# Attention's stores of x behind its loads, a new order within a batch, and ranks, lanes and scatter positions at other places

## The chip, the core and the metric

The kernel runs on one core of one Trainium2 chip. The metric is the device time of one execution in microseconds (us). Engines: TensorE (PE, its weight loads PEld), VectorE (DVE), ScalarE (ACT), GpSimd (POOL) and SyncE (SP, which here issues DMAs).

## What is computed

```python
# q, k, v: (8, 8, 576, 64); the attention has no softmax
kv = einsum('bhsd,bhse->bhde', k, v)
out = einsum('bhsd,bhde->bhse', q, kv)
x = out / sqrt(mean(out * out, -1) + 1e-6) * g_norm     # -> x: (4608, 512), one row per token
logits = x @ w_gate + modality_bias[modality_id]        # 8 experts
e_idx = argmax(logits, axis=1)
for e in range(8):                                      # F = 1024
    h = relu(x[e_idx == e] @ w1[e])
    y[e_idx == e] = gate_w[e_idx == e] * (h @ w2[e])
gate = 1 / (1 + exp(-(y @ w_gate2)))
result = (gate * (y @ w_val)) @ w_out                   # d_ff = 1536
```

## The kernel before, in words

There are three stages. Attention (lines 141 to 519) makes x, chooses each token's expert and numbers the tokens by expert. The expert stage (589 to 832) gathers the rows of x by that numbering, in 26 items of one or two tiles of 128 tokens, and multiplies them with w1 and w2. The last stage (836 to 953) is the gated pair of products. All matrix products but the routing's counts are in full precision, made of split high and low parts.

The order is written out by hand: each engine executes its instructions in the order of the code, and waits at an instruction whose data or buffer is not there. SP's queue issues nearly all loads and stores, in the order of the code too.

Attention works batch by batch (line 376). For batch b, `emit_kv` (234) makes the product of k and v on PE ("kv", 72 products) and VectorE copies it into a block R. `emit_RT` (247) transposes R on PE into PSUM (rtp), VectorE copies that to SBUF (rt), and `emit_M` (254) multiplies rt with the router's weights (mp) and copies the result into the last 16 columns of R. `emit_qT` (261) transposes a quarter of q (qc, a copy of q in another layout; in odd batches a fifth piece qr with the rest of two batches), and ScalarE copies it to one of five qT buffers. `emit_out` (269) multiplies qT with R: x not yet normed and the router's raw logits at once; ScalarE copies it to o and squares it (sq), VectorE sums the squares (ssq). The outputs of batch b are made while batch b+1 is under way, piece r by piece r. One pass of the loop before:

- kv of batch b at the start, then for each r: out(b-1, r), the transposition of R (r = 0), qT(b, r), M (r = 2);
- loads of batch b+2 at r = 1, `norm` (286) of batch b-2 and the store of x of batch b-4 (`store_x`, 368);
- in odd passes `choose` (309: expert of each token as a one-hot, oh), in the even pass after the next odd one `rank` (323: the place of each token within its expert, by matmuls of oh with a triangle and with ones), `lanes` (350: a one-hot of the place within 128, lo) and `numbers` (357: lo times the token's number, two rows of lid per tile).

The loads' buffers are double: k and v of batch b+2 can be loaded when kv(b) has read them. The x buffers o are three for even and two for odd batches. A DMA on SP's or ScalarE's queue has one of eight semaphores in turn, and waits until the DMA eight places before it has landed.

Behind the loop come the last norm, choose and rank, then (439 to 503) a chain of small instructions on VectorE that turns the experts' counts into a code for each of 44 slots (sc); its comparison with each token's code (soh) and 72 products with lid (ph) give the token that stands in each place of a slot. From that come gidx (492), the rows that the gathers read, and est (503), the experts of the items. Lines 508 to 519 make sidx, the rows that the scatters of y write; the first scatter comes when the first item is done. `split_w` and line 438 split weights into high part (ScalarE, w1h) and low part (VectorE, w1l, 486).

Of the kernel before, what the change touches and what calls it, by code (L numbers as in the profile page):

```python
# [23 lines left out]
E = 8  # L24
# [10 lines left out]
C_U, C_IOTA, C_TOK, C_DESC, C_POS, C_REST, C_ITEM, C_CODE, C_ID, C_W = 0, 128, 256, 328, 336, 380, 381, 407, 432, 560  # L35
# [11 lines left out]
def shape_constants():  # L47
# [12 lines left out]
    c[:, C_TOK:C_TOK + NTILE] = (tok + 1) // 128  # L60
# [4 lines left out]
    e = 160 - NTILE * (E - np.arange(E))  # L65
    c[:, C_CODE:C_CODE + 18] = [*e, 200, *e, 200]
# [5 lines left out]
def attention_moe_glu_kernel(  # L72
# [68 lines left out]
    with ExitStack() as st:  # L141
# [29 lines left out]
        code = big.tile([128, NTILE], BF16, name="code")  # L171
# [21 lines left out]

        load_kv(0)
# [5 lines left out]
        load_q(0)  # L200
        load_kv(1)
        load_q(1)
# [13 lines left out]
        nc.vector.memset(onesb, 1.0)  # L216
        nc.vector.memset(tot[:, 0, :], 0.0)
# [14 lines left out]
        qT, o_t, me_t = {}, {}, {}  # L232
# [76 lines left out]
        def choose(bp):  # L309
# [4 lines left out]
            me = me_t[bp] = sm.tile([128, 9], F32, tag="me", name="me")  # L314
# [8 lines left out]
        def rank(bp):  # L323

            t0, n = 9 * bp, 9
            og = oh[:, t0:t0 + n, :]
            tr = sm.tile([128, 8], F32, tag="tr", name="tr")
            nc.vector.tensor_reduce(out=tr, in_=og.rearrange("p t e -> p e t"), op=ALU.add, axis=AX)
            nc.vector.tensor_tensor(out=tot[:, bp + 1, :], in0=tot[:, bp, :], in1=tr, op=ALU.add)
# [20 lines left out]
        def lanes(bp, lane):  # L350

            bc = [128, 9, 128]
            lo = wk.tile(bc, BF16, tag="lo", name="lo", bufs=1)
            nc.vector.tensor_tensor(out=lo, in0=iotab.unsqueeze(1).broadcast_to(bc), in1=lane.unsqueeze(2).broadcast_to(bc), op=ALU.is_equal)
            return lo

        def numbers(bp, lo, act):

            t0, n, bc = 9 * bp, 9, [128, 9, 128]
            for w in range(2):  # L360
                c = w * NTILE + t0
                if act:
                    for t in range(n):
                        nc.scalar.activation(out=lid[:, t0 + t, w, :], in_=lo[:, t, :], func=ACTF.Copy, scale=ct[:, C_TOK + c + t:C_TOK + c + t + 1])
                else:
                    nc.gpsimd.tensor_tensor(out=lid[:, t0:t0 + n, w, :], in0=lo, in1=tokb[:, c:c + n].unsqueeze(2).broadcast_to(bc), op=ALU.mult)
# [9 lines left out]
        for b in range(B + 1):  # L376
            if b < B:
                qc = wk.tile([128, 4, H, D], F32, tag="qc", name="qc", bufs=1)
                nc.scalar.activation(out=qc[:, 0], in_=q_t[b][:, :, 0, :], func=ACTF.Copy)
                emit_kv(b)  # L380
            if b == 0:
                make_bias()
            for r in range(5):
                if b == B and r == 0:
                    ld_scope.close()
                    mw = [mw_scope.enter_context(tc.tile_pool(name="m_wr0", bufs=1, side="right", reuse_waits="tile"))]
                    w1p = w1_scope.enter_context(tc.tile_pool(name="m_w1", bufs=3, side="right", reuse_waits="tile"))
                    w1r = [mw[0].tile([128, KC, F1], F32, tag="w1r0", name="w1r0")]
                    w2r = [mw[0].tile([128, F1 // 128, DM], F32, tag="w2r0", name="w2r0")]
                    nc.sync.dma_start(out=w1r[0], in_=w1[0].rearrange("(c p) f -> p c f", p=128))  # L390
                if b < B and r == 0:
                    nc.scalar.activation(out=qc[:, 1], in_=q_t[b][:, :, 1, :], func=ACTF.Copy)
                    for i in (2, 3):
                        nc.gpsimd.tensor_copy(out=qc[:, i], in_=q_t[b][:, :, i, :])
                if b:
                    emit_out(b - 1, r)
                if b < B:
                    if r == 0:
                        emit_RT(b)
                    if r < 4:  # L400
                        emit_qT((b, r), qc[:, r].rearrange("p h d -> p (h d)"))
                    elif b % 2:
                        emit_qT((b, 4), qr_t[b // 2].rearrange("p h d -> p (h d)"))
                    if r == 2:
                        emit_M(b)
                if r == 1:
                    load_kv(b + 2)
                    load_q(b + 2)
                    if b > 1:
                        norm(b - 2)  # L410
                    if b > 3:
                        store_x(b - 4)
                if b % 2 and b > 1:
                    if r == 3:
                        choose(b // 2 - 1)
                elif b > 2:
                    if r == 1:
                        lane = rank(b // 2 - 2)
                    elif r == 3:
                        lo = lanes(b // 2 - 2, lane)  # L420
                        if b < B:
                            numbers(b // 2 - 2, lo, False)
# [5 lines left out]
        numbers(2, lo, True)  # L428
# [5 lines left out]
        nc.tensor.matmul(out=tp, lhsT=onesb, rhs=tot[:, 4, :], start=True, stop=True)  # L434
        numbers(3, lanes(3, lane), True)
        w1s = {(0, 0): [w1p.tile([128, KC, 256], F32R, tag="w1" + z, name="w1" + z) for z in "hl"]}
        wq = w1r[0][:, :, 0:256]
        nc.scalar.activation(out=w1s[0, 0][0], in_=wq, func=ACTF.Copy)
        ti = big.tile([128, 8], I32, name="ti")
        tw = big.tile([128, 2, 8], I32, name="tw")  # L440
        seg = big.tile([128, 18], F32, name="seg")
        off = big.tile([128, 18], F32, name="off")
        dlt = big.tile([128, 17], F32, name="dlt")
        cnt = big.tile([128, 17], F32, name="cnt")
        pad = big.tile([128, 17], F32, name="pad")
        cmp, cm2 = (wk.tile([128, 512], F32, tag="rt", name=z)[:, 0:NITEM * 17].rearrange("p (t g) -> p t g", g=17) for z in ("cmp", "cm2"))
        itc, itp = (big.tile([128, NITEM], F32, name=z) for z in ("itc", "itp"))
        sc = big.tile([128, NSLOT], BF16, name="sc")
# [25 lines left out]
        for i in range(2):  # L474
            nc.vector.tensor_scalar(out=pairs[:, :, i], in0=itc[:, 0:NPAIR], scalar1=float(i), scalar2=None, op0=ALU.add)
        nc.vector.tensor_copy(out=sc[:, 2 * NPAIR:], in_=itc[:, NPAIR:])
        ph = [pq.tile([128, 512], F32, tag="q", name="php") for _ in range(2)]
        for t0 in range(0, NTILE, 9):
# [8 lines left out]
        vv = big.tile([128, NSLOT], F32, name="vv")  # L487
        v1 = big.tile([128, NSLOT], F32, name="v1")
        v2 = big.tile([128, NSLOT], F32, name="v2")
# [17 lines left out]

# [3 lines left out]
        nc.vector.tensor_tensor(out=pad, in0=seg[:, 1:18], in1=seg[:, 0:17], op=ALU.subtract)  # L511
        nc.vector.scalar_tensor_tensor(out=pad, in0=pad, scalar=128.0, in1=cnt, op0=ALU.mult, op1=ALU.subtract)
        nc.vector.tensor_tensor(out=cm2, in0=cmp, in1=pad.unsqueeze(1).broadcast_to([128, NITEM, 17]), op=ALU.mult)
        nc.vector.tensor_reduce(out=itp, in_=cm2, op=ALU.add, axis=AX)
        pos, v1p = (z[:, 0:2 * NPAIR].rearrange("p (t i) -> p t i", i=2) for z in (ct[:, C_POS:C_POS + NSLOT], v1))
# [464 lines left out]
```

## Time and profile before

| | us |
|---|---|
| median of 3 runs | 1585.08 (1582.66 to 1587.09) |
| the profiled execution | 1581.24, its span 1579.5 |
| kv of batch 0 starts on PE | 12.98 |
| first out of batch 7 on PE | 120.51 |
| last norm starts on VectorE | 132.62 |
| gidx is ready | 149.89 |
| first gathered tile is normed | 154.53 |
| PE busy over the span | 1509.2 (96%) |

The profile is of one execution; times inside it count from the start of its span. Busy time is that in which the engine executes; the granted clock (PEclk) is a mean over a stretch, 1.00 for 2.4 GHz throughout. A releaser is what the profile takes for the end of a wait; "issue" stands where it shows none. Durations on VectorE and ScalarE overlap a little with the next instruction's start.

### The profile page before, as it was taken

The page shows a single profiled execution, that of the slowest core. Times are in us where ns is not written, and L with a number is a line of the kernel's source. Part 1 is how long each engine was busy: PE and PEld are TensorE (multiplying, and loading weights), DVE is VectorE, ACT ScalarE, POOL GpSimd, SP SyncE. Part 2 cuts the span into 40 slices and gives each one's busy share as a digit, 9 for nine tenths or more (in the row PEclk, how much of TensorE's full clock was granted, in tenths as well). Part 3 has the DMA queues.
Part 4 walks back from the last instruction along what each step waited for, and adds up shares of the span by engine and source line. Part 5 has one row for each costly group of instructions (what it writes and reads, how often), then busy time and mean ns, then how long its engine had stood idle before and what let it go on. Part 6 is the DMA issues. An engine that isn't in the chain of part 4 may idle for free.

```text
span 1579.5 us, 22828 instructions
## 1 busy us (share of the span) xinstructions
PE 1509.2 (96%) x9089; PEld 1298.1 (82%) x9089; DVE 839.0 (53%) x1306; ACT 716.0 (45%) x1147; POOL 380.7 (24%) x418
## 2 busy tenths in 40 slices
PE   6993999999999999989999999999999999999997
PEld 6982899999999999767888888888888888888885
DVE  2558778878878878575333433333333333333322
ACT  3755555555555556533333433333333343333332
POOL 1031112222222213131311414114132141231211
PEclk9996999999999999999999999999999999999999
DMA  9976787757784778350000000000000000000000
GB/s 304 334 273 229 197 281 272 283 190 276 266 308 164 264 269 289 134 209 28 27 1 28 27 28 27 1 28 28 26 29 1 28 27 1 27 1 1 27 1 27
DMA packets 78877, 195.86 MB, mean 124 GB/s; under 512 B 13872, under 2 KB 22320, under 8 KB 75824
## 3 DMA queue, kind: packets, MB, share of 16 engines
q1 hardware_dynamic: 63984, 153.55, 28.5%
q0 software_dynamic: 12064, 40.46, 7.1%
q8 instruction: 74, 1.21, 0.3%
q10 hardware_dynamic: 2720, 0.35, 0.2%
q14 instruction: 35, 0.29, 0.1%
HBM read 177.08 MB, written 38.23 MB: 136 GB/s over the span
## 4 chain that ended last, share of the span: by engine, by line
PE 89%; DMA 4%; DVE 4%; issue 1%; ACT 1%; POOL 1%; POOLq 0%; SPq 0%; DVEq 0%; ACTq 0%
PE gv L576 12%; PE gv L578 12%; PE gv L577 12%; PE ac L895 6%; PE ac L897 6%; PE ac L896 6%; PE ph L672 5%; PE ph L671 5%; PE ph L670 5%; PE py L692 5%; PE py L693 5%; PE py L694 4%; PE kv L241 2%; PE ops L278 2%; DMA y_d<-y,sidx 2%; PE xtp L655 1%
## 5 line engine op out<-in xcount | busy, mean ns | idle before, releaser
L576 PE MATMUL gv<-yh,gvh 128*128 128x512 f32 x848 | 336.0, 396 | 0.0
L578 PE MATMUL gv<-yh,gvl 128*128 128x512 f32 x848 | 332.6, 392 | 2.0 <-DVE gvl L570 2.0
L577 PE MATMUL gv<-yl,gvh 128*128 128x512 f32 x848 | 331.2, 391 | 0.0
L580 DVE TENSOR_TENSOR gm<-sg,gv 128x512 f32<-128x512 f32 x107 | 73.5, 687 | 411.8 <-PE gv L578 410.1
L873 POOL TENSOR_TENSOR wol<-wlast,woh 128x512 fp32r<-128x512 f32 x72 | 100.0, 1389 | 475.0 <-ACT woh L872 475.0
L581 ACT ACTIVATE gh<-gm 128x512 fp32r<-128x512 f32 x107 | 67.6, 632 | 312.1 <-DVE gm L580 312.1
L670 PE MATMUL ph<-xh,w1h 128*128 128x256 f32 (+1 forms) x704 | 201.9, 287 | 0.8 <-ACT xh L659 0.8
L672 PE MATMUL ph<-xl,w1h 128*128 128x256 f32 (+1 forms) x704 | 199.5, 283 | 0.0
L671 PE MATMUL ph<-xh,w1l 128*128 128x256 f32 (+1 forms) x704 | 199.2, 283 | 0.0
L578 PEld LDWEIGHTS gv<-yh,gvl 128*128 128x128 f32 x848 | 159.5, 188 | 38.4 <-DVE gvl L570 2.9
L577 PEld LDWEIGHTS gv<-yl,gvh 128*128 128x128 f32 x848 | 159.7, 188 | 33.3
L576 PEld LDWEIGHTS gv<-yh,gvh 128*128 128x128 f32 x848 | 160.0, 189 | 32.1
L895 PE MATMUL ac<-woh,gh 128*128 128x512 f32 x428 | 168.2, 393 | 0.0
L897 PE MATMUL ac<-woh,gl 128*128 128x512 f32 x428 | 167.9, 392 | 0.0
L896 PE MATMUL ac<-wol,gh 128*128 128x512 f32 x428 | 166.7, 390 | 0.0
L579 ACT ACTIVATE sg<-gv 128x512 f32<-128x512 f32 x107 | 63.9, 597 | 166.2 <-PE gv L578 166.2
L670 PEld LDWEIGHTS ph<-xh,w1h 128*128 128x128 f32 x704 | 135.9, 193 | 2.9 <-ACT xh L659 1.2
L671 PEld LDWEIGHTS ph<-xh,w1l 128*128 128x128 f32 x704 | 136.0, 193 | 1.7
L672 PEld LDWEIGHTS ph<-xl,w1h 128*128 128x128 f32 x704 | 135.8, 193 | 0.3 <-DVE xl L660 0.3
L692 PE MATMUL py<-w2h,hh 128*128 128x512 f32 x320 | 126.8, 396 | 0.5 <-ACT w2h L637 0.5
L693 PE MATMUL py<-w2l,hh 128*128 128x512 f32 x320 | 125.7, 393 | 0.8 <-DVE w2l L638 0.8
L694 PE MATMUL py<-w2h,hl 128*128 128x512 f32 x320 | 124.9, 390 | 0.0
(218 smaller groups left out, 2486.9 us busy)
## 6 DMA issues: line engine op xcount, KB each, us to landing
w1r<-in_moe_w_dram SPq DMA_DIRECT2D x23, 2048.0 KB, 9.4
w2r<-in_moe_w_dram SPq DMA_DIRECT2D x23, 2048.0 KB, 10.4
kt<-in_k_dram SPq DMA_DIRECT2D x8, 1152.0 KB, 8.8
vt<-in_v_dram SPq DMA_DIRECT2D x8, 1152.0 KB
x_d<-o SPq DMA_DIRECT2D x8, 1152.0 KB
yr<-y_d SPq DMA_DIRECT2D x8, 1056.0 KB, 4.8
qt<-in_q_dram SPq DMA_DIRECT2D x8, 1024.0 KB, 10.3
w_d<-d_f SPq DMA_DIRECT2D x28, 256.0 KB, 8.5
```

The source lines that it names most:

```text
L576: nc.tensor.matmul(out=ps[m], lhsT=h[:, m, c, :], rhs=yh[:, :, c, :], start=(c == 0), stop=False)
L577: nc.tensor.matmul(out=ps[m], lhsT=h[:, m, c, :], rhs=yl[:, :, c, :], start=False, stop=False)
L578: nc.tensor.matmul(out=ps[m], lhsT=l[:, m, c, :], rhs=yh[:, :, c, :], start=False, stop=(c == KC - 1))
L670: nc.tensor.matmul(out=o, lhsT=bh[:, c, cs], rhs=hi[:, c, 0:n], start=(c == 0), stop=False)
L671: nc.tensor.matmul(out=o, lhsT=bl[:, c, cs], rhs=hi[:, c, 0:n], start=False, stop=False)
L672: nc.tensor.matmul(out=o, lhsT=bh[:, c, cs], rhs=lo[:, c, 0:n], start=False, stop=(c == KC - 1))
L692: nc.tensor.matmul(out=o, lhsT=hi[:, f, cs], rhs=bh[:, f, :], start=first, stop=False)
L693: nc.tensor.matmul(out=o, lhsT=hi[:, f, cs], rhs=bl[:, f, :], start=False, stop=False)
L694: nc.tensor.matmul(out=o, lhsT=lo[:, f, cs], rhs=bh[:, f, :], start=False, stop=last)
L895: nc.tensor.matmul(out=o, lhsT=gh[:, cs], rhs=wh, start=(j == 0), stop=False)
L896: nc.tensor.matmul(out=o, lhsT=gh[:, cs], rhs=wl, start=False, stop=False)
L897: nc.tensor.matmul(out=o, lhsT=gl[:, cs], rhs=wh, start=False, stop=(j == NJ - 1))
```

## The change

Loads and stores: q of a batch is loaded ahead of its k and v, and loads of batch b+2 are issued behind kv(b). The stores of x of batches 0 to 3 move behind all loads (passes 6 and 7). Both kinds of o buffers are three.

The pass: pairs of qT(b, r) and out(b-1, r) with the transposition first, kv behind the third pair, the transposition of R at r = 3, M at r = 4. All copies of q stand at the pass's start.

Ranks: `rank` stands in the same odd pass as `choose`, `lanes` and `numbers` in the next even pass, all on GpSimd. A base term (128 x 36 x expert) goes into rank's sum on PE, so the code is place minus lane, in F32. For the last two batches VectorE makes no lo: ScalarE makes each lane's distance (Abs) and then Relu(c - c x distance), which is c where the distance is 0 and 0 elsewhere. Token numbers come in one sum: the high parts are stored times 128, and both rows go to one PSUM tile.

Positions: the instructions that make sidx move behind the first item's transpositions in the expert stage, with their constants in a tile of their own (posl, a load on SP).

```diff
+        load_q(0)
         load_kv(0)
...
-        load_q(0)
+        load_q(1)
         load_kv(1)
-        load_q(1)
...
-                o_t[b] = wk.tile([128, 4 + b % 2, XW], F32, tag=f"o{b % 2}", name="o", bufs=3 - b % 2)
+                o_t[b] = wk.tile([128, 4 + b % 2, XW], F32, tag=f"o{b % 2}", name="o", bufs=3)
...
-            nc.tensor.matmul(out=ps, lhsT=ubf, rhs=og, start=True, stop=False)
+            nc.tensor.matmul(out=ps, lhsT=onesb, rhs=base, start=True, stop=False)
             nc.tensor.matmul(out=ps, lhsT=onesb, rhs=tot[:, bp, :].unsqueeze(1).broadcast_to([128, n, 8]), start=False, stop=False)
+            nc.tensor.matmul(out=ps, lhsT=ubf, rhs=og, start=False, stop=False)
...
-            nc.vector.tensor_scalar(out=rt, in0=ri, scalar1=7, scalar2=None, op0=ALU.arith_shift_right)
-            nc.vector.tensor_tensor(out=code[:, t0:t0 + n], in0=me, in1=rt, op=ALU.add)
+            nc.vector.tensor_tensor(out=code[:, t0:t0 + n], in0=rf, in1=lane, op=ALU.subtract)
...
+        def numbers_last(lane):
+
+            for t in range(9):
+                lo = wk.tile([128, 128], BF16, tag="lt", name="lt")
+                nc.scalar.activation(out=lo, in_=iotab, func=ACTF.Abs, scale=-1.0, bias=lane[:, t:t + 1])
+                for w in range(2):
+                    c, m = C_TOK + w * NTILE + 27 + t, C_NEG + 9 * w + t
+                    nc.scalar.activation(out=lid[:, 27 + t, w, :], in_=lo, func=ACTF.Relu, scale=ct[:, m:m + 1], bias=ct[:, c:c + 1])
...
             for r in range(5):
...
                 if b < B:
-                    if r == 0:
-                        emit_RT(b)
                     if r < 4:
                         emit_qT((b, r), qc[:, r].rearrange("p h d -> p (h d)"))
                     elif b % 2:
                         emit_qT((b, 4), qr_t[b // 2].rearrange("p h d -> p (h d)"))
+                if b:
+                    emit_out(b - 1, r)
+                if b < B:
                     if r == 2:
+                        emit_kv(b)
+                        load_q(b + 2)
+                        load_kv(b + 2)
+                    elif r == 3:
+                        emit_RT(b)
+                    elif r == 4:
                         emit_M(b)
                 if r == 1:
-                    load_kv(b + 2)
-                    load_q(b + 2)
                     if b > 1:
                         norm(b - 2)
-                    if b > 3:
-                        store_x(b - 4)
+                    for c in {6: (0, 1), 7: (2, 3), 8: (4,)}.get(b, ()):
+                        store_x(c)
                 if b % 2 and b > 1:
-                    if r == 3:
+                    if r == 2:
                         choose(b // 2 - 1)
-                elif b > 2:
-                    if r == 1:
-                        lane = rank(b // 2 - 2)
-                    elif r == 3:
-                        lo = lanes(b // 2 - 2, lane)
-                        if b < B:
-                            numbers(b // 2 - 2, lo, False)
+                    elif r == 4:
+                        lane = rank(b // 2 - 1)
+                elif b > 2 and r == 1:
+                    numbers(b // 2 - 2, lane)
...
-                    nc.tensor.matmul(out=ph[w][:, 0:NSLOT], lhsT=lid[:, t, w, :], rhs=soh[:, t, :],
-                                     start=(t == 0), stop=(t == NTILE - 1))
+                    nc.tensor.matmul(out=ph, lhsT=lid[:, t, w, :], rhs=soh[:, t, :], start=(t + w == 0), stop=(t + w == NTILE))
         nc.vector.tensor_tensor(out=w1s[0, 0][1], in0=wq, in1=w1s[0, 0][0], op=ALU.subtract)
...
-        nc.vector.tensor_scalar(out=v1, in0=ph[0][:, 0:NSLOT], scalar1=128.0, scalar2=-1.0, op0=ALU.mult, op1=ALU.add)
-        nc.vector.tensor_tensor(out=vv, in0=v1, in1=ph[1][:, 0:NSLOT], op=ALU.add)
-        nc.vector.tensor_scalar(out=gidx, in0=vv, scalar1=0.0, scalar2=None, op0=ALU.max)
+        nc.vector.tensor_scalar(out=gidx, in0=ph, scalar1=-1.0, scalar2=0.0, op0=ALU.add, op1=ALU.max)
+        nc.vector.tensor_copy(out=vv, in_=ph)
...
             for i in range(2):
                 emit_A(lo, i)
+            if sure:
+                positions()
```

Three places in the instruction order. The first is PE in pass 5 from its kv on (R_128 is the R of batch 4 or 5, qps a transposition of q, ops an out product); before:

```order
L241 MATMUL kv<-vt,kt 64x64 x72
L278 MATMUL ops<-R_127,qT 128x144 x4
L250 MATMUL rtp<-ident,R_128 128x128 x4
L264 MATMUL qps<-ident,qc 128x128 x4
L278 MATMUL ops<-R_127,qT 128x144 x4
L264 MATMUL qps<-ident,qc 128x128 x4
L278 MATMUL ops<-R_127,qT 128x144 x4
L264 MATMUL qps<-ident,qc 128x128 x4
L258 MATMUL mp<-wpt,rt 128x16 x4
```

And PE in pass 5 now, from the third pair on:

```order
L267 MATMUL qps<-ident,qc 128x128 x4
L281 MATMUL ops<-R_128,qT 128x144 x4
L244 MATMUL kv<-vt,kt 64x64 x72
L267 MATMUL qps<-ident,qc 128x128 x4
L281 MATMUL ops<-R_128,qT 128x144 x4
L253 MATMUL rtp<-ident,R_129 128x128 x4
L267 MATMUL qps<-ident,qr 128x128 x4
L261 MATMUL mp<-wpt,rt 128x16 x4
L335 LDWEIGHTS onesb
```

Five pieces stood between the transposition of R (rtp) and M (mp), and one (qr) stands there now; the out piece that stood behind kv now has a transposition in front. The second place is VectorE in the same pass, from the copies of kv on; before:

```order
L242 COPY R_128<-kv 64x4x64
L243 COPY R_128<-kv 64x4x64
L284 TENSOR_REDUCE ssq<-sq 128x8
L252 COPY rt<-rtp 128x512
L284 TENSOR_REDUCE ssq<-sq 128x8
L293 TENSOR_SCALAR ssq<-ssq 128x40
```

And VectorE now:

```order
L245 COPY R_129<-kv 64x4x64
L246 COPY R_129<-kv 64x4x64
L320 TENSOR_REDUCE mx<-lg 128x9
L321 TENSOR_TENSOR eq<-lg,mx 128x72
L322 TENSOR_TENSOR eq<-eq,ct 128x72
L323 TENSOR_REDUCE me<-eq 128x9
L324 TENSOR_TENSOR oh<-me,ct 128x72
L287 TENSOR_REDUCE ssq<-sq 128x8
L255 COPY rt<-rtp 128x512
L262 COPY R_129<-mp 128x4x16
```

In both the copy to rt stands right behind the ssq of the out piece that follows kv; choose (mx to oh) has come in front of it in odd passes. The third place is ScalarE behind the last norm's root (rt<-ssq); before:

```order
L294 ACTIVATE rt<-ssq 128x40
L364 ACTIVATE lid<-lo,ct 128x128 x36
L438 ACTIVATE w1h<-w1r_1685 128x1024
L506 ACT_TABLE_LOAD
L506 ACTIVATE ex<-ex 128x288
```

And now, the end of the nine groups of three:

```order
L364 ACTIVATE lt<-iotab,lane 128x128
L367 ACTIVATE lid<-lt,ct 128x128 x2
L441 ACTIVATE w1h<-w1r_1712 128x1024
L507 ACT_TABLE_LOAD
L507 ACTIVATE ex<-ex 128x288
```

Of the 36 pieces before, 18 were of batches 4 and 5; those are GpSimd's now, and batches 6 and 7 take 27 pieces, each second one of a group reading what the first wrote.

## Rows read from the trace of the kernel before

**Rows 1.** Windows: us; busy of PE, PEld, DVE, ACT, POOL; PEclk, DMA share, GB/s
```profile
120.00:160.00 40.00, 12.60 (x152) 10.87 (x153) 32.96 (x111) 22.93 (x56) 8.38 (x10) 0.62 0.65 232
```

**Rows 2.** Timeline of PE, batch 0: start, duration, instruction [idle before <-releaser]
```profile
12.98 6.27 PE L241 MATMUL kv<-vt,kt 64*64 64x64 f32 x144 [12.98 <-DMA vt<-in_v_dram]
20.30 0.63 PE L250 MATMUL rtp<-ident,R 128*128 128x128 f32 x4 [1.05 <-DVE R L243]
```

**Rows 3.** Waits of PE: who waited for whom, us in total, times, longest
```profile
PE kv L241 <- issue: 4.9, 2, 3.2
```

**Rows 4.** Timeline of PE, passes 6 to 8
```profile
101.52 0.35 PE L334 MATMUL rkp<-oh,onesb 128*128 128x64 bf16 x8
...
107.17 4.41 PE L241 MATMUL kv<-vt,kt 64*64 64x64 f32 x144
111.51 1.25 PE L278 MATMUL ops<-R,qT 128*128 128x144 f32 x8
...
113.47 1.15 PE L278 MATMUL ops<-R,qT 128*128 128x144 f32 x8
...
115.87 0.60 PE L264 MATMUL qps<-ident,qc 128*128 128x128 f32 x4
116.31 0.96 PE L258 MATMUL mp<-wpt,rt 128*128 128x16 f32 x8
117.12 1.23 PE L278 MATMUL ops<-R,qT 128*128 128x144 f32 x8
...
120.51 2.23 PE L278 MATMUL ops<-R,qT 128*128 128x144 f32 x16 [1.07 <-DVE R L259]
```

**Rows 5.** Timeline of SP's queue, the first load of q
```profile
7.83 0.37 SPq L188 DMA_DIRECT2D qt<-in_q_dram  x1
```

**Rows 6.** Timeline of ScalarE, the first copy of q
```profile
17.09 0.63 ACT L379 ACTIVATE qc<-qt 128x512 f32<-128x512 f32 x1 [6.10 <-DMA qt<-in_q_dram]
```

**Rows 7.** Timeline of VectorE, the copy to rt in pass 7
```profile
114.86 0.69 DVE L252 COPY rt<-rtp 128x512 f32<-128x512 f32 x1
```

**Rows 8.** Timeline of VectorE, last pass to the first gathered tiles
```profile
127.68 0.28 DVE L328 TENSOR_REDUCE tr<-oh 128x8 f32<-128x72 bf16 x1
...
129.46 1.27 DVE L284 TENSOR_REDUCE ssq<-sq 128x8 f32<-128x512 f32 x2
...
132.62 0.18 DVE L293 TENSOR_SCALAR ssq<-ssq 128x40 f32<-128x40 f32 x1
...
138.64 0.18 DVE L345 CAST lane<-rl 128x9 bf16<-128x9 int32 x1
...
139.00 1.35 DVE L354 TENSOR_TENSOR lo<-iotab,lane 128x1152 bf16<-128x1152 bf16 x1
...
147.67 1.22 DVE L486 TENSOR_TENSOR w1l<-w1r,w1h 128x1024 fp32r<-128x1024 f32 x1
...
149.70 0.19 DVE L492 TENSOR_SCALAR gidx<-vv 128x44 int32<-128x44 f32 x1
...
152.11 0.17 DVE L511 TENSOR_TENSOR pad<-seg 128x17 f32<-128x17 f32 x1
...
154.53 0.69 DVE L647 TENSOR_TENSOR xg<-xg 128x512 f32<-128x512 f32 x1
156.22 0.69 DVE L647 TENSOR_TENSOR xg<-xg 128x512 f32<-128x512 f32 x1 [1.00 <-DMA xg<-x_d,gidx]
```

**Rows 9.** Timeline of ScalarE, the last lanes' rows and the first split
```profile
140.39 5.36 ACT L364 ACTIVATE lid<-lo,ct 128x128 bf16<-128x128 bf16 x18 [2.06 <-DVE lo L354]
145.65 1.04 ACT L438 ACTIVATE w1h<-w1r 128x1024 fp32r<-128x1024 f32 x1
```

**Rows 10.** Groups by line and shape: busy us, mean ns | idle before
```profile
L364 ACT ACTIVATE lid<-lo,ct 128x128 bf16<-128x128 bf16 x36 | 10.7, 386 | 2.1 <-DVE lo L354 2.1
```

**Rows 11.** Windows of 4 us around and behind PE's unexplained waits, columns as in Rows 1
```profile
52.00:56.00 4.00, 2.31 (x51) 2.11 (x48) 1.03 (x3) 0.62 (x2) 0.00 (x0) 1.00 1.06 367
96.00:100.00 4.00, 4.00 (x40) 3.88 (x38) 0.84 (x2) 0.63 (x1) 0.00 (x0) 0.62 1.03 427
```

More of the change, by code (lines that the diff above doesn't have):

```diff
@@ L64, in shape_constants @@
     c[:, C_REST] = NT + p
-    e = 160 - NTILE * (E - np.arange(E))
-    c[:, C_CODE:C_CODE + 18] = [*e, 200, *e, 200]
+    e = NTILE * np.arange(E)
+    c[:, C_CODE:C_CODE + 18] = [*e, 400, *e, 400]
+    c[:, C_NEG:C_NEG + 18] = -c[:, [C_TOK + w * NTILE + 27 + t for w in range(2) for t in range(9)]]
     c[:, C_ITEM:C_ITEM + NITEM] = [first_slot(t) for t in range(NITEM)]
@@ L170, in attention_moe_glu_kernel @@
         tot = big.tile([128, 5, 8], BF16, name="tot")
-        code = big.tile([128, NTILE], BF16, name="code")
+        code = big.tile([128, NTILE], F32, name="code")
+        base = big.tile([128, 9, 8], BF16, name="base")
         lid = big.tile([128, NTILE, 2, 128], BF16, name="lid")
@@ L216, in attention_moe_glu_kernel @@
         nc.vector.memset(onesb, 1.0)
+        nc.vector.tensor_scalar(out=base, in0=ct[:, C_CODE:C_CODE + 8].unsqueeze(1).broadcast_to([128, 9, 8]), scalar1=ct[:, C_U + 1:C_U + 2], scalar2=128.0, op0=ALU.mult, op1=ALU.mult)
         nc.vector.memset(tot[:, 0, :], 0.0)
@@ L378, in attention_moe_glu_kernel @@
                 qc = wk.tile([128, 4, H, D], F32, tag="qc", name="qc", bufs=1)
-                nc.scalar.activation(out=qc[:, 0], in_=q_t[b][:, :, 0, :], func=ACTF.Copy)
-                emit_kv(b)
-            if b == 0:
+                for r in (0, 1):
+                    nc.scalar.activation(out=qc[:, r], in_=q_t[b][:, :, r, :], func=ACTF.Copy)
+                for r in (2, 3):
+                    nc.gpsimd.tensor_copy(out=qc[:, r], in_=q_t[b][:, :, r, :])
+            else:
+                ld_scope.close()
+                mw = [mw_scope.enter_context(tc.tile_pool(name="m_wr0", bufs=1, side="right", reuse_waits="tile"))]
+                w1p = w1_scope.enter_context(tc.tile_pool(name="m_w1", bufs=3, side="right", reuse_waits="tile"))
+                late = w1_scope.enter_context(tc.tile_pool(name="m_late", bufs=1, side="right", reuse_waits="tile"))
+                w1r = [mw[0].tile([128, KC, F1], F32, tag="w1r0", name="w1r0")]
+                w2r = [mw[0].tile([128, F1 // 128, DM], F32, tag="w2r0", name="w2r0")]
+                nc.sync.dma_start(out=w1r[0], in_=w1[0].rearrange("(c p) f -> p c f", p=128))
+            if b == 1:
                 make_bias()
             for r in range(5):
[L384 to L396, printed above, removed]
                 if b < B:
-                    if r == 0:
-                        emit_RT(b)
                     if r < 4:
@@ L433, in attention_moe_glu_kernel @@
         tp = pkv.tile([128, 8], F32, tag="kv", name="totp")
-        nc.tensor.matmul(out=tp, lhsT=onesb, rhs=tot[:, 4, :], start=True, stop=True)
-        numbers(3, lanes(3, lane), True)
+        nc.tensor.matmul(out=tp, lhsT=onesb, rhs=tot[:, 3, :], start=True, stop=False)
+        for t in range(27, NTILE):
+            nc.tensor.matmul(out=tp, lhsT=onesb, rhs=oh[:, t, :], start=False, stop=(t == NTILE - 1))
+        numbers_last(lane)
         w1s = {(0, 0): [w1p.tile([128, KC, 256], F32R, tag="w1" + z, name="w1" + z) for z in "hl"]}
+        posl = late.tile([128, NSLOT + 1], F32, name="posl")
+        nc.sync.dma_start(out=posl, in_=cst[:, C_POS:C_POS + NSLOT + 1])
         wq = w1r[0][:, :, 0:256]
@@ L439, in attention_moe_glu_kernel @@
         ti = big.tile([128, 8], I32, name="ti")
-        tw = big.tile([128, 2, 8], I32, name="tw")
-        seg = big.tile([128, 18], F32, name="seg")
+        tw = late.tile([128, 2, 8], I32, name="tw")
+        seg = late.tile([128, 18], F32, name="seg")
         off = big.tile([128, 18], F32, name="off")
         dlt = big.tile([128, 17], F32, name="dlt")
[L444 to L448, printed above, removed]
+        cnt = late.tile([128, 17], F32, name="cnt")
+        pad = late.tile([128, 17], F32, name="pad")
+        cmp, cm2 = (late.tile([128, NITEM, 17], F32, name=z) for z in ("cmp", "cm2"))
+        itc, itp = (late.tile([128, NITEM], F32, name=z) for z in ("itc", "itp"))
+        sc = big.tile([128, NSLOT], F32, name="sc")
         soh = big.tile([128, NTILE, NSLOT], BF16, name="soh")
@@ L474, in attention_moe_glu_kernel @@
         for i in range(2):
-            nc.vector.tensor_scalar(out=pairs[:, :, i], in0=itc[:, 0:NPAIR], scalar1=float(i), scalar2=None, op0=ALU.add)
-        nc.vector.tensor_copy(out=sc[:, 2 * NPAIR:], in_=itc[:, NPAIR:])
-        ph = [pq.tile([128, 512], F32, tag="q", name="php") for _ in range(2)]
+            nc.vector.tensor_scalar(out=pairs[:, :, i], in0=itc[:, 0:NPAIR], scalar1=float(i), scalar2=128.0, op0=ALU.add, op1=ALU.mult)
+        nc.vector.tensor_scalar(out=sc[:, 2 * NPAIR:], in0=itc[:, NPAIR:], scalar1=128.0, scalar2=None, op0=ALU.mult)
+        ph = pq.tile([128, 512], F32, tag="q", name="php")[:, 0:NSLOT]
         for t0 in range(0, NTILE, 9):
```

61 lines of the change are left out of this document (26 added, 35 removed).

## The prediction

> **What bounds the kernel now.** I read the windows first, then PE's timeline in attention, then the chain from the last batch to the first expert matmul, and last the waits of PE and SP. The change lies before 170 us. Behind that PE is busy nearly all the time in both kernels, so what counts is when the first expert matmul starts. The window to see is 120 to 160 us: PE works 12.60 of 40 us and its granted clock is 0.62 on average [rows 1]. Ahead of it PE bounds attention: it starts at 12.98 when the first v lands [rows 2], and from then to the first output product of batch 7 at 120.51 it waits little. Its largest waits are two in the k-v products that no engine releases, 4.9 us together, the longer 3.2 [rows 3]. One batch is a row of PE pieces [rows 4]: the k-v product ("kv") 4.34 us (107.17 to 111.51), two pairs of an output product ("out") and a q transposition 2.84 us (113.47 to 116.31), so 1.42 a pair with 0.44 (115.87 to 116.31) for the transposition, and the small product M 0.81 us (116.31 to 117.12). From 120.51 the chain goes over VectorE and ScalarE to the index that the gathers need (gidx, ready at 149.89) [rows 8], and from there to PE.
>
> So I ask two things: when does out(7,0) start, and how long is it from there to gidx?
>
> **The start of attention.** q of batch 0 now goes ahead of k and v. In the kernel before the queue issued q only at 7.83 us, after k and v, and q had landed at 17.09, when ScalarE could copy it [rows 5, 6]. k, v and q of a batch move the same bytes in any order, so I let the last of the three land at the same 17.1 and kv(0) start there. Both ends: 12.98, if q costs nothing, and 19, if SP's queue stands still for 2 us in between. Three transpositions move into that wait. kv(0) takes 6.27 us as before, the transposition of R starts 1.05 us behind it and takes 0.63 [rows 2]; the copy to rt takes 0.69 [rows 7] and M 0.81. Batch 1 starts at 17.1 + 6.3 + 3.1 = 26.5.
>
> **One batch.** The new order on PE is three pairs, kv, a fourth pair, the transposition of R, the fifth piece, M. Three pairs and kv take 3 x 1.42 + 4.34 = 8.60 us. What decides is the way from kv's end to M. Before, five pieces of work lay between the transposition of R and M; now one piece does. And VectorE takes the copy to rt, on which M waits, only behind the squares' sum (ssq) of the out piece that PE did just after kv. The kernel before has the same chain, hidden: out starts at 111.51, then ScalarE's copy to o and its squares, then ssq, then rt, done at 114.86 + 0.69 = 115.55 [rows 4, 7], 4.04 us in all. PE got to M at 116.31 and never waited. In the changed order the out piece starts 0.44 behind kv and follows a transposition (1.15 us instead of 1.25 [rows 4]): 0.44 + 3.94 = 4.38 us from kv to M, then 0.81. PE's own pieces in that stretch (pair 1.42, R 0.5, q rest 0.44) are 2.4 us, so it waits 2.0 us for rt.
> - Odd batches: 8.60 + 5.19 = 13.8, and the rank matmuls now behind M, 0.3 (eight of them are 0.35 long, overlapped [rows 4]): 14.1.
> - Even batches: there are five qT buffers, and the fourth copy qT(b,3) takes the buffer that out(b-1,3) reads; ScalarE's order puts that copy ahead of o, so the chain grows by one copy, 0.5 us (ScalarE's copy of 128x512 is 0.63 long [rows 6], less the overlap with the next). 14.3; the wait for M is about 1.9, since the fifth out piece of 1.1 lies in front of it.
>
> The sum: 26.5 + 13.8 (batch 1) + 3 x 14.1 + 3 x 14.3 = 125.5 for out(7,0), against 120.51 [rows 4]: +5.0. The 6.6 us that PE lost in the kernel before, in the unexplained waits (4.9) and to the clock behind the longer one (about 1.5, below), I take as gone: PE now pauses in each batch, and loads have gaps since kv(b) frees their buffers later than they could use them. If those waits return, they come on top.
>
> **Stores, ranks, buffers.** The stores of x of batches 0 to 3 now stand behind the last load; nothing waits for them but the gathers, which come 50 us later, and a third o buffer per parity carries the wait: price 0, up to 2 us if out(6,0) meets store 0. Rank of batches 4 and 5 leaves the last pass. There VectorE ran it from 127.68 to 129.46, 1.78 us, right on the chain between out(7,0) and the last norm at 132.62 [rows 8]. That stretch shrinks from 12.1 to 10.3 us: the last norm starts at 135.8, +3.2. The base term and the tile numbers scaled by 128 change counts, not lengths; the sum tr, tot and me of the last rank (0.6 us) ran beside PE's rank matmuls, which set rk, so 0. The lane of the last rank is ready 6.2 us behind the norm's start (138.82 before), unchanged.
>
> **Last lanes on ScalarE.** Before, from lane to gidx: 138.82 to 149.89, 11.1 us, with VectorE's lo of 1.27 us in it (from 139.00; it is 1.35 long, the next instruction starts a little earlier than its end) [rows 8]. Without lo VectorE and PE would need 9.8. But ScalarE now has 27 pieces instead of 18: 18 take 5.36 us, 0.298 each, when they overlap [rows 9], and 0.386 when one must be complete [rows 10]. Of each three, one depends on the one in front of it: 0.41 + 2 x 0.298 = 1.0, nine times 9.0. Behind them stands the first split of w1 on ScalarE (1.04 [rows 9]), behind it w1l on VectorE (1.22 [rows 8]), and VectorE takes gidx (0.19) after w1l: 9.0 + 1.04 + 1.2 + 0.2 + 0.1 of hops = 11.6. So +0.5, not -1.3. Bounds: 27 x 0.298 = 8.0 gives -0.5, 27 x 0.41 = 11.1 gives +2.6. I take 11.6, since the dependence is in the order.
>
> **Behind gidx.** The nine instructions for scatter positions took VectorE from 152.11 to 154.53, and the first product by 1/rms followed without a wait; but the second waited 1.00 us for its gather, at 156.22 [rows 8]. PE needs both. So moving them gains 0 at the first matmul; at their new place the first item's first matmuls hide them, and if those don't, 2.4 us return.
>
> Sum: +3.2 at the last norm, +0.5 to gidx: +3.7. On the profiled execution (1581.24) this is 1584.9; that execution lies 3.8 below the median of 1585.1, so for the median I give 1585.1 + 3.7 = **1588.8**. A measurement of this kernel can tell 0.3%, 4.8 us; the forecast lies just inside it.
>
> **Rivals.**
> - *The clock falls in the new waits.* Behind the 3.2 us wait PE's granted clock was 0.62 from 96 to 100 us, that is, part of it at the lower of the two levels, 1.2 GHz [rows 11]: 4 x 0.38 = 1.5 us lost. The other unexplained wait, 1.7 us (4.9 less 3.2), lies between 52 and 56 us, and there the clock stayed at 1.00, all at 2.4 GHz. The new waits of 1.9 to 2.0 are nearer to the one that cost nothing. If each costs the clock, 7 x 1.5 = 10.5: 1599.3. Chance 0.12. [...]
> - *The unexplained waits return* on top of the waits for M: + 4.9 to + 6.4, 1593.7 to 1595.2. For it: each kv still issues its 144 matmuls in 4.3 us. Against: loads no longer fill every gap. Chance 0.17.
> - *No wait for M* (faster): if the copy to rt doesn't stand behind ssq in time, since ScalarE and VectorE are early, PE runs at its own pieces: 7 waits of 1.9 to 2.0, 13.5 us, go: 1575.3; it is faster by over 0.3% when more than 8.5 of the 13.5 go. Against it: the out piece that feeds ssq is issued after kv, so nobody can be early. For it: PE was never made to wait at this place before. Chance 0.18.
> - The forecast itself: 0.50, its own range 1585 to 1593 (start of kv(0) by 2 us, ScalarE's chain by 1, the way to M by 2). The rest, 0.03, lies between the cases.
>
> The range that takes in the rivals up to 2 in 10 is 1578 to 1600. Faster by over 0.3%: 0.18. Slower: the first two rivals (0.29) and the upper third of the forecast (0.15): 0.44. Within 0.3%: 0.38.
>
> **What would show it.** In the trace after: kv(0) near 17 us; in each of batches 1 to 7 a wait of about 2 us ahead of M, released by VectorE's copy to rt, with ssq right in front of that copy; batches 14 us apart; out(7,0) at about 125.5; no rank between out(7,0) and the last norm; 27 small pieces on ScalarE in about 9 us, and w1l right ahead of gidx. I am wrong if PE doesn't wait ahead of M, if the batches stay 12.5 us apart, or if a mean granted clock well below 1 stands in the windows from 40 to 110 us.

## The result, and the profile after

The changed kernel takes 1601.07 us (median of 4 runs, 1599.04 to 1602.36), the kernel before 1583.87 on the same chips: ratio 1.0104, 95% interval 1.0084 to 1.0125. The forecast was 1588.8, range 1578 to 1600. The profiled execution has a span of 1600.1 us against 1579.5, 20.6 more. The starts of six instructions in both traces divide that:

| from ... to | before | after | forecast | measured |
|---|---|---|---|---|
| start ... out(7,0) | 120.51 | 134.35 | +5.0 | +13.8 |
| ... last norm | 12.11 | 11.96 | -1.8 | -0.2 |
| ... last lane | 6.02 | 7.07 | 0 | +1.1 |
| ... gidx | 11.06 | 13.32 | +0.5 | +2.3 |
| ... first expert matmul | 9.16 | 8.42 | 0 | -0.7 |
| ... second item's transposition | 12.79 | 16.26 | 0 | +3.5 |
| ... end | 1407.85 | 1408.72 | 0 | +0.9 |

The waits of PE in attention, after (who waited for whom, us in total, times, longest), for [rows 3]:

```profile
PE mp L261 <- DVE rt L255: 12.1, 8, 2.0
PE kv L244 <- DMA vt<-in_v_dram: 2.8, 1, 2.8
PE rtp L253 <- DVE R L246: 1.5, 3, 0.9
PE kv L244 <- issue: 1.1, 2, 0.5
```

The wait ahead of M is there, 11.3 us without batch 0's, and the two pauses that no engine releases have shrunk from 4.9 to 1.1. PE's timeline, for [rows 2, 4]; the last four rows are the first experts:

```profile
18.18 5.92 PE L244 MATMUL kv<-vt,kt 64*64 64x64 f32 x144 [2.83 <-DMA vt<-in_v_dram]
...
31.90 4.30 PE L244 MATMUL kv<-vt,kt 64*64 64x64 f32 x140
36.74 0.33 PE L244 MATMUL kv<-vt,kt 64*64 64x64 f32 x4 [0.54 <-issue]
...
41.48 1.42 PE L261 MATMUL mp<-wpt,rt 128*128 128x16 f32 x8 [1.97 <-DVE rt L255]
...
43.62 2.04 PE L281 MATMUL ops<-R,qT 128*128 128x144 f32 x8
...
73.61 1.06 PE L261 MATMUL mp<-wpt,rt 128*128 128x16 f32 x8 [1.97 <-DVE rt L255]
...
75.30 1.15 PE L281 MATMUL ops<-R,qT 128*128 128x144 f32 x8
...
132.97 1.06 PE L261 MATMUL mp<-wpt,rt 128*128 128x16 f32 x8 [1.97 <-DVE rt L255]
...
134.35 5.79 PE L281 MATMUL ops<-R,qT 128*128 128x144 f32 x32
...
175.12 0.58 PE L673 MATMUL ph<-xh,w1h 128*128 128x256 f32 x1 [0.78 <-ACT xh L662]
...
185.26 0.70 PE L695 MATMUL py<-w2h,hh 128*128 128x512 f32 x1 [2.42 <-ACT w2h L640]
186.51 0.80 PE L696 MATMUL py<-w2l,hh 128*128 128x512 f32 x1 [0.56 <-DVE w2l L641]
187.11 0.63 PE L697 MATMUL py<-w2h,hl 128*128 128x512 f32 x1
```

Compare the out pieces behind two waits of the same 1.97 us: 2.04 us at 43.62, 1.15 at 75.30. The granted clock tells why. Windows of 2 us, columns as in [rows 1]:

```profile
42.00:44.00 2.00, 2.00 (x11) 2.00 (x11) 0.22 (x1) 0.00 (x0) 0.00 (x0) 0.51 1.06 376
...
60.00:62.00 2.00, 2.00 (x10) 1.99 (x10) 0.00 (x0) 0.55 (x1) 0.00 (x0) 0.50 1.04 342
...
134.00:136.00 2.00, 1.98 (x19) 1.88 (x17) 1.64 (x9) 0.00 (x0) 0.00 (x0) 0.55 0.96 211
...
190.00:192.00 2.00, 2.00 (x7) 1.51 (x7) 1.46 (x2) 0.00 (x0) 0.00 (x0) 0.50 0.90 260
```

0.50 is the lower level, 1.2 GHz. It came behind three of the seven waits for M and behind the longer wait for w2h, where a matmul of 128x512 takes 0.63 us instead of 0.39.

VectorE from the last pass to the gathered tiles, for [rows 8], then GpSimd, then ScalarE, for [rows 9]:

```profile
140.99 0.19 DVE L299 TENSOR_TENSOR tt<-rsq 128x32 f32<-128x32 f32 x1
...
144.16 1.27 DVE L287 TENSOR_REDUCE ssq<-sq 128x8 f32<-128x512 f32 x2
...
146.31 0.18 DVE L296 TENSOR_SCALAR ssq<-ssq 128x40 f32<-128x40 f32 x1
...
147.23 1.32 DVE L299 TENSOR_TENSOR tt<-rsq 128x40 f32<-128x40 f32 x1
...
153.38 0.17 DVE L347 CAST lane<-rl 128x9 f32<-128x9 int32 x1
...
166.70 0.20 DVE L492 TENSOR_SCALAR gidx<-php 128x44 int32<-128x44 f32 x1
```
```profile
144.32 4.17 POOL L358 TENSOR_TENSOR lid<-lo,tokb 128x1152 bf16<-128x1152 bf16 x2 [1.90 <-DVE lo L355]
```
```profile
153.59 0.40 ACT L364 ACTIVATE lt<-iotab,lane 128x128 bf16<-128x128 bf16 x1 [6.83 <-DVE lane L347]
154.02 0.88 ACT L367 ACTIVATE lid<-lt,ct 128x128 bf16<-128x128 bf16 x2
...
164.43 1.04 ACT L441 ACTIVATE w1h<-w1r 128x1024 fp32r<-128x1024 f32 x1
```

No rank stands between out(7,0) and the last norm. But the product tt, 0.20 us in the kernel before, takes 1.32: it ends at 148.55, when GpSimd's two lid instructions end (148.49). And ScalarE's 27 pieces take 10.84 us (153.59 to 164.43). SyncE's queue, behind the gathers:

```profile
171.10 12.63 SPq L617 DMA_DIRECT2D w1r<-in_moe_w_dram  x2
184.07 5.01 SPq L617 DMA_DIRECT2D w2r<-in_moe_w_dram  x2
```

Item 0's w2 stands behind both w1, of items 0 and 1, and is issued only at 184.07; ScalarE's w2h, for which PE waits, starts right behind it.

### The profile page after: what moved, and what is told of

The parts are those of the page before. It is cut to its first block, busy times and chain, and to the rows that moved or that the text cites. A ratio compares the mean times of both kernels' runs of the same rounds, so it can differ in the third digit from the quotient of the medians.

```text
span 1600.1 us, 22830 instructions
## 1 busy us (share of the span) xinstructions
PE 1518.1 (95%) x9102; PEld 1302.3 (81%) x9102; DVE 840.4 (53%) x1295; ACT 716.8 (45%) x1138; POOL 387.0 (24%) x420
## 3 DMA queue, kind: packets, MB, share of 16 engines
q8 instruction: 74, 1.21, 0.3%
## 4 chain that ended last, share of the span: by engine, by line
PE 88%; DMA 5%; DVE 3%; issue 2%; ACT 1%; POOL 1%; SPq 0%; POOLq 0%; ACTq 0%; DVEq 0%
PE gv L567 12%; PE gv L569 12%; PE gv L568 11%; PE ac L900 6%; PE ac L902 6%; PE ac L901 6%; PE ph L675 5%; PE ph L674 5%; PE ph L673 5%; PE py L695 5%; PE py L696 5%; PE py L697 4%; PE kv L244 2%; PE ops L281 2%; DMA y_d<-y,sidx 2%
```

## The experiments

Each is the changed kernel with the edit shown. Ratios are to the kernel before, run on the same chip. Attention alone differs by up to 4.5 us between profiled executions with the same attention code: out(7,0) starts at 134.35 in the changed kernel, at 137.68 in e3 and at 138.84 in e4. So small effects are read in their own stretch of the trace, and the +13.8 of the table is the least of three: e3 and e4 lose 17.2 and 18.3 there.

**e1: take the wait for rt away.** RT ahead of the out piece:

```
             if r < 4: emit_qT(...)
+            if r == 3: emit_RT(b)
         if b: emit_out(b - 1, r)
         ...
-            elif r == 3: emit_RT(b)
```


> The changed kernel with one move: the transposition of R is issued ahead of the out piece behind kv, so VectorE's copy to rt stands ahead of that piece's ssq. Theory (rt behind ssq makes PE wait): the 12 us of waits ahead of M go, a wait of 0.4 us for the copies of R comes ahead of the transposition in each batch; M comes 2.9 us behind kv instead of 4.5 to 5.0, some 10 us in seven batches, and up to 5 us more if the clock no longer falls behind the waits: 1586 to 1591. Rival (the loads set the pace, and the wait would only move to the k-v product): the batches stay 14.4 to 15 us apart and the time 1600.

1602.2 us, ratio 1.0098 (1.0075 to 1.0121): the rival's number. PE's waits from 13 to 140 us:

```profile
PE qps L267 <- ACT qc L381: 5.8, 6, 1.5
PE rtp L253 <- DVE R L246: 5.8, 8, 1.9
...
PE mp L261 <- DVE rt L255: 1.4, 3, 0.8
```

The wait for rt fell from 12.1 to 1.4 us, and as much stands elsewhere: PE waits 5.8 us for ScalarE's copy of the next q, which stands behind o and its squares, and 5.8 instead of 1.5 for R. So the wait that I had named was real, and not the bound.

**q1: that copy too.** As e1, and q of batch b+1 copied in batch b (two buffers):

```
+                    if r == 3: copy_q(b + 1)
```


> e1 (the transposition of R ahead of the out piece) and ScalarE's copies of the next batch's q moved half a pass ahead, into a second buffer; the k-v product stays in the middle of the pass. Theory (two chains of like length close the circle of a batch: over ssq and rt to M, and over the out pieces and the copy of q to the next transposition): with both cut, PE waits 0.4 to 1 us in a batch, batches lie 12.6 to 13.3 us apart: 1584 to 1590. Rival (any order with the k-v product in the middle is slow since ScalarE has too little time): PE waits for the q copies or for o instead, over 14 us: 1600.

1600.5, ratio 1.0113 (1.0094 to 1.0131). The wait for the copy of q is gone, but:

```profile
PE ops L281 <- DVE R L262: 7.1, 5, 2.5
PE rtp L253 <- DVE R L246: 5.5, 8, 1.9
```

Now out waits for VectorE's copy of M, behind two ssq (L287). The starts of kv lie 13.4 to 13.8 us apart behind odd batches and 16.9 to 17.9 behind even ones from batch 2 on. The rival's number holds, with VectorE where I had named q or o.

**p1: the old pass order.** kv at the start, each out piece ahead of its transposition, RT behind the first out piece, M behind the third transposition, the loads of batch b+2 at r = 1; q ahead of k and v, stores and rank as changed.

```
+                emit_kv(b)
...
+                    if r == 0: emit_RT(b)
+                    elif r == 2: emit_M(b)
```


> The changed kernel with the pass of a batch in the old order again (k-v product at its start, the transposition of R behind the first out piece, M behind the third transposition), all else as changed. e1 took away the wait for rt and PE then waited for ScalarE's copy of q instead. Theory (the k-v product stood where it covered ScalarE's copies at the change of batches, and both waits come from its move): neither wait shows, batches lie 12.5 to 13 us apart instead of 14.3 to 16.2, kv(0) still starts near 18, out(7,0) comes near 125 instead of 134.4: 1590 to 1593. Rival (the order of loads and stores sets the pace): the batches stay over 14 us apart, 1600.

1593.6, ratio 1.0051 (1.0035 to 1.0067), 0.6 above the range, with out(7,0) at 127.6. This edit puts the whole order back, so what kv's place does by itself is not shown. None of the waits of e1 or q1 is left. What is there instead comes with the early rank:

```profile
PE rkp L335 <- ACT qT L269: 3.1, 3, 1.0
PE rkp L337 <- DVE oh L324: 3.0, 3, 1.0
```

**p4: rank and numbers back too.**

```
-                    elif r == 4: lane = rank(b // 2 - 1)
+                elif b > 2 and r == 1: lane = rank(b // 2 - 2)
```


> p1 with the rank and the numbers of a pair of batches back in the next even pass. In p1 PE waited 1.0 us for a qT copy and 1.0 for the one-hot (oh) ahead of each of three ranks. Theory (the early rank costs PE 2 us three times in the old pass order, and saves VectorE 1.8 us once, in the last pass): 6.1 less in attention, 1.8 more behind it: 1588.5 to 1590.5. Rival (the waits for oh lie where PE would have waited anyway, for o or for loads): 1593 to 1595.5.

1591.6, ratio 1.0043 (1.0029 to 1.0058), 1 above the range; those waits are gone. out(7,0) starts at 125.45: 8.9 us earlier than in the changed kernel (12.2 and 13.4 earlier than in e3 and e4), 4.9 later than before [rows 4], with kv(0) at 17.57, 4.6 later than before. So most of what attention lost is pass order and place of rank; the 4.9 that stay are nearly the later start of kv(0), with q ahead of k and v.

**e2: the early start alone.** k, v ahead of q, kv(0) ahead of its transpositions.

```
-        load_q(0)
         load_kv(0)
+            if b == 0: emit_kv(b)
```


> The changed kernel with k and v of batch 0 loaded ahead of q again, and the k-v product of batch 0 ahead of its transpositions. Theory: kv(0) starts at 13.0 instead of 18.2, the first M some 4.7 us earlier and everything behind it too: 1596.4. Rival (loads of later batches set the pace, so an early start only waits later): 1601, with new waits for loads in batches 2 and 3.

1603.2, ratio 1.0115 (1.0099 to 1.0132): nothing comes of it. PE's timeline:

```profile
12.33 7.08 PE L244 MATMUL kv<-vt,kt 64*64 64x64 f32 x144 [12.33 <-DMA vt<-in_v_dram]
...
30.33 4.30 PE L244 MATMUL kv<-vt,kt 64*64 64x64 f32 x140 [1.75 <-DMA vt<-in_v_dram]
37.62 0.33 PE L244 MATMUL kv<-vt,kt 64*64 64x64 f32 x4 [3.00 <-issue]
```

The 5.9 us won at the start were gone in batch 1: kv(0) took 1.2 longer, 1.75 went into the wait for batch 1's v, and 3.00 into a pause that was 0.54 in the changed kernel, at the same matmul; kv of batch 2 starts at 48.42, in the changed kernel at 48.43.

**e3: ScalarE's pieces reordered.** All Abs, then all Relu.

```
+            for t in range(9): nc.scalar.activation(out=los[t], ..., func=ACTF.Abs, ...)
             for t in range(9): ... func=ACTF.Relu ...
```


> The changed kernel with all nine Abs pieces of the last lanes ahead of the eighteen Relu pieces, each in its own buffer. Theory of the prediction (a piece is slow only where it reads what the piece in front of it wrote): 27 pieces take 8.1 to 8.5 us instead of 10.8, gidx comes 2.3 to 2.8 earlier: 1598.5. Rival (each piece with a bias operand takes 0.40 us by itself, whatever is in front of it): 10.8 us as before and 1601.

1601.3, ratio 1.0104 (1.0087 to 1.0121). ScalarE's timeline:

```profile
156.91 2.73 ACT L364 ACTIVATE lt<-iotab,lane 128x128 bf16<-128x128 bf16 x9 [6.83 <-DVE lane L347]
159.55 7.01 ACT L369 ACTIVATE lid<-lt,ct 128x128 bf16<-128x128 bf16 x18
```

9.56 us in place of 10.84 (the next instruction starts at 166.47), and gidx comes 12.04 us behind the lane instead of 13.32; the time doesn't show it, with attention 3.3 us longer in this execution. The truth is between: Abs now takes 0.29 apiece, so the dependence costs 1.3 us; the Relu pieces, with a scale and a bias operand, take 0.39 with nothing to wait for. The Trainium skill, ScalarE: Activation LUTs, section "What ACT_TABLE_LOAD costs", says that each per-partition operand lengthens an ACTIVATE by some 93 ns; the trace agrees: 0.39 here, 0.298 for the copy with a scale alone [rows 9].

**e4: positions in front again.**

```
             split_w(lo, 0, 0)
+            if sure: positions()
             for i in range(2): norm_x(lo, i)
```


> The changed kernel with the nine instructions of the scatter positions back in front of the first products by 1/rms. Theory (the 0.74 us that the move brings to the first expert matmul is given back at PE's wait for w2h, which GpSimd's load of w1 sets, and that longer wait costs the clock): the first expert matmul comes 0.7 us later, the wait for w2h is 0.5 to 1.7 instead of 2.4, the clock need not fall behind it: 1597.5 to 1601. Rival (the move is a plain gain): 1601.8 to 1603.5.

1602.4, ratio 1.0108 (1.0091 to 1.0125). From gidx (170.77) to the first expert matmul (179.40) 8.63 us instead of 8.42. That is no gain that can be told: with the positions moved, as in the changed kernel, this stretch takes 8.52 in e2 and 9.43 in q1, and 9.16 in the kernel before. The wait for w2h was 1.1, as the theory had it, but the clock fell behind it again.

**e7: stores in their old place.**

```
-                    for c in {6: (0, 1), 7: (2, 3), 8: (4,)}.get(b, ()): store_x(c)
+                    if b > 3: store_x(b - 4)
```


> The changed kernel with each store of x four batches behind its product again instead of behind the last load. Theory (the stores' place costs nothing and gains nothing, since nothing waits for them): 1600 to 1602, the circle of a batch unchanged. Rival (stores among the loads crowd the transfers): pauses in the k-v products of more than 1 us, and v late, 1603 to 1606.

1601.8, ratio 1.0106 (1.0091 to 1.0120): neither cost nor gain.

**t1: four edits behind attention.**

```
-                elif b > 2 and r == 1:
+                elif b > 2 and r == (0 if b == B else 1):      # numbers
...
+ lanes 0 to 2: comparison and ACTF.Copy; 3 to 8: all ACTF.Abs, then ACTF.Relu
+ w1l issued behind est
-            for which in range(2):
-                for t in range(lo, lo + ahead):
+            for t in range(lo, lo + ahead):
+                for which in range(2):
```


> The changed kernel with four edits behind attention, each with a stretch of its own: the numbers of batches 4 and 5 at the start of the last pass (GpSimd done before the last norm's product tt); of the last lanes three by VectorE's comparison and ScalarE's copy, six by all Abs and then all Relu; the split w1l on VectorE behind the index; the loads of w1 and w2 item by item. Theory: tt takes 0.2 instead of 1.3 us; ScalarE's chain 8.3 instead of 10.8 and gidx 10.0 us behind the lane instead of 13.3; PE's wait for w2h of 2.4 us goes and with it the low clock behind it (3 us): 1590 to 1593. Rival for the wait: it is the bytes that are late, not the order of the queue: then the wait stays or grows as gidx comes earlier, 1594 to 1597.

1597.2, ratio 1.0087 (1.0069 to 1.0105), above the forecast. What the edits aimed at came: last norm to lane 5.95 us (7.07), lane to gidx 9.69 (13.32), and neither a wait for w2h nor the low clock behind it. But the first edit, the earlier numbers, cost elsewhere what it brought. VectorE, then GpSimd:

```profile
141.71 1.71 DVE L296 TENSOR_SCALAR ssq<-ssq 128x32 f32<-128x32 f32 x1
...
144.11 1.39 DVE L299 TENSOR_TENSOR tt<-rsq 128x32 f32<-128x32 f32 x1
...
150.28 0.20 DVE L299 TENSOR_TENSOR tt<-rsq 128x40 f32<-128x40 f32 x1
...
155.31 0.17 DVE L347 CAST lane<-rl 128x9 f32<-128x9 int32 x1
...
165.00 0.20 DVE L498 TENSOR_SCALAR gidx<-php 128x44 int32<-128x44 f32 x1 [1.44 <-PE php L494]
```
```profile
141.28 4.18 POOL L358 TENSOR_TENSOR lid<-lo,tokb 128x1152 bf16<-128x1152 bf16 x2 [12.45 <-DVE lo L355]
```

The collision left the last norm and met the one before it, twice (1.71 and 1.39 us instead of about 0.2), each time until one of GpSimd's instructions of 2.1 us ended; out(7,0) to the last norm grew from 11.96 to 13.7 us. The Trainium skill, SBUF — State Buffer, section "Who interferes with whom", names an exclusive lock on a port pair that the two engines share; the trace agrees for these operations, while the reductions (ssq at 144.16 in the changed kernel) ran on beside it.

**p2, p3: together.** p2 is p1, t1 and k, v of batches 0 and 1 ahead of q.

> p1 and t1 together, and k and v of batch 0 loaded ahead of q. Theory: what p1 and t1 bring adds up, and the start at 12.5 to 13 brings 4 us more, since the pass in the old order has slack for late loads no less than the kernel before: 1575 to 1579, under the 1583.6 of the kernel before. Rival (as in e2 an early start is lost again to loads and to pauses in the k-v products): 1580 to 1584.

1589.9, ratio 1.0028 (1.0012 to 1.0044), above both forecasts: kv(0) at 12.54, but v of batch 2 came 3.28 us late and a pause of 2.86 followed. I put that down to the later loads, which still had q in front. p3 has all loads, the pass order, rank and the numbers of batches 4 and 5 as before, and the rest of t1.

> All that the runs speak for: pass order, load order and place of rank as in the kernel before; the numbers of batches 4 and 5 on ScalarE as there; from the change the held-back stores, the one-sum index and the moved positions; from t1 three of the last lanes over VectorE's comparison and six by all Abs and then all Relu, the split w1l behind the index, the loads of w1 and w2 item by item. Theory: attention as before (out(7,0) near 120.5 to 122), gidx 9.7 us behind the lane instead of 11.1, no wait for w2h (1.2 us before): 2.5 to 3.5 under the kernel before, 1580 to 1581.5. Rival (what is gained ahead of the first expert matmul is lost to its gathers and to the clock): 1583 to 1585.

**1577.4 us, ratio 0.9961 (0.9945 to 0.9978)**: faster than both, and 2.6 under the forecast. Its twelve times lay in two groups (eight of 1573 to 1580, four of 1585 to 1586), and the profiled one, of the upper group, has these pauses:

```profile
39.99 1.73 PE L244 MATMUL kv<-vt,kt 64*64 64x64 f32 x50 [0.41 <-issue]
...
55.30 0.73 PE L244 MATMUL kv<-vt,kt 64*64 64x64 f32 x17 [1.33 <-issue]
...
82.13 3.99 PE L244 MATMUL kv<-vt,kt 64*64 64x64 f32 x78 [2.62 <-issue]
...
101.17 1.98 PE L244 MATMUL kv<-vt,kt 64*64 64x64 f32 x32 [3.77 <-issue]
```


> The same kernel as p3_best, once more with a profile. Its twelve times lay in two groups, 1573 to 1580 and 1585 to 1586, and the profiled one was of the upper group, with 8.1 us of pauses in the k-v products that no engine releases. Theory (the pauses make the groups): a time under 1580 goes with pauses of 2 us or less in sum, a time near 1585 with 5 to 8 us of them, at the same four places in the order of PE's instructions. Rival (the groups come from behind attention, as the clock in the first experts): pauses alike, and the difference stands behind 160 us.

That run took 1582.6 on a chip where the kernel before took 1591.7, one run of each, with pauses of 1.69 and 4.08. It was no run of the lower group's kind, so the theory on the groups stays open: pauses of 5.8 in place of 8.1 us go with a span 3.4 shorter, no more is shown. From out(7,0) to the second item's transposition the two traces of p3 take 47.2 and 47.0 us, the kernel before 51.1: that gain is seen. Their out(7,0) came at 127.2 and 124.2 instead of 120.5, so attention was slower in both, and what makes the lower group fast stands in no trace.

## Why the prediction was wrong

The wait ahead of M came as forecast, and the +3.7 us still became +20.6 in the profiled execution, 16.9 more. The step that failed first is that the new waits would not cost the clock: they cost 3.4 us ahead of out(7,0) and 1.4 behind it. The other terms were put at nothing or too small: in attention the start, the pauses and small terms (5.5), behind it GpSimd's numbers beside the last norm (1.1), ScalarE's pieces (1.8) and the wait for w2h with the low clock behind it (3.5). The rest, 0.2, is small differences.

- *The wait for M*: right. I said 2.0 us in odd and 1.9 in even batches, by VectorE's copy behind ssq; it is 1.97 and 0.6 to 1.4. But it is not the only chain that holds a batch at this length: without it the time stayed (e1), since others are nearly as long. The step "What decides is the way from kv's end to M" followed one chain and not the others. In the old order no such wait is left (p1). My reading is that kv, which needs loads and a free R but nothing else from ScalarE or VectorE, covered ScalarE's copies at the change of batches and covers them no more in the middle of a pass; its place was not tested by itself.
- *Batches of 14.1 and 14.3*: between batches 4 and 7, where the clock stood at 1.00, kv's starts lie 14.4 to 15.5 apart. In batches 1 to 3 the lower clock took 3.4 more (M 0.35, three pairs 5.69 and 6.12 us instead of 4.39). Against the forecast of out(7,0), 125.5, the 8.9 us are: the start 0.9 (batch 1 at 27.4, not 26.5), the clock 3.4, two pauses with what they lengthen 1.5, and 3.1 of many small terms, 0.3 to 0.7 in each batch.
- *"The new waits are nearer to the one that cost nothing"*: wrong. The rival on the clock had a chance of 0.12 and took all seven waits alike. Three of seven cost it: the clock well below 1 between 40 and 110 us was one of the signs that I had named. Of the third, 1.4 us stand behind out(7,0), in out pieces of 5.79 us, and ate most of the 1.8 that the rank's leaving brought. In e1 and q1 these pieces ran at the higher level (4.44 and 4.49 us), and that stretch took 10.6 and 10.7 us, near my 10.3, instead of 11.96.
- *The pauses go*: mostly, 1.1 instead of 4.9.
- *ScalarE's 27 pieces, 9.0 us*: mis-sized; 10.84, near my upper bound of 11.1. I took 0.298 for two of three pieces, from a copy with one operand, where the Relu pieces have two and take 0.39 (e3).
- *The numbers of batches 4 and 5 on GpSimd*: I had given them no price. They cost the last norm 1.1 us.
- *Behind gidx, 0*: right for the positions, as far as e4 can tell. But I stopped at the first expert matmul. There PE met a longer wait for w2h (2.42 instead of 0.48), and the low clock behind it: +3.5. SyncE's queue shows whose wait it is, and t1 takes it away: item 0's w2 stood behind item 1's w1, which waits for GpSimd's transfer into the same buffer. But its size differs from one execution to the next: in e3 and e7, with the same code there, the wait was 0.7 us and the stretch 13.1 and 12.4 us, hardly more than the 12.79 before. Those two had lost 17 us in attention instead.
- *Stores*: right, 0 (e7).

## What to carry to other kernels

When a wait is the newest thing in a trace, ask what closes the loop a little behind it: cut it in thought, and follow each other chain once around before saying what it costs. A long product that needs only loads may be worth most where the other engines are behind; moving it can uncover them all at once, as I read p1. And take the duration of an instruction from one with the same operands, and follow a gain past the point at which you measure it, to the next wait.

## What the runs showed of the hardware

The pauses that no engine releases stand at fixed places in PE's order. Counting matmuls from the start: behind 727 and 1359 in the kernel before; 348 and 978 in the changed kernel, e1, e2 and e4; 474, 727, 1105 and 1359 in p3. All lie multiples of 126 apart (within 3), whatever work stands there, and the transfers just before the changed kernel's first (34 to 35 us) show an instruction packet (q8) while the engines are full:

```profile
q1 hardware_dynamic: 175, 0.37, 100.2%
q8 instruction: 1, 0.02, 6.9%
```

The profile's page counts 74 such packets with 1.21 MB, 16 KB each; PE has 9102 matmuls and as many weight loads, so one packet comes to 123 matmuls, close to the 126. In the kernel before, such packets stand in 51 to 53 and 91 to 93 us, where its two pauses begin (52.8 and 92.2). So I read the pauses as PE waiting for its own instructions behind the loads, 0.3 to 4.1 us; that was not tested by itself. The Trainium skill, Runtime: NRT & Kernel Launch, section "Instruction fetch mechanics", has blocks of that size and calls the cost of crossing one mostly hidden; if my reading holds, it is not hidden here where loads fill the queues. The low clock behind a wait of 2 us was not settled either: of equal waits of 1.97 us some cost it and some did not.
